# Attention's first tiles: r and k loaded without empty partitions, one v tile first, two products on VectorE, masks written ahead of the next tile's sums

## The chip, the cores and the metric

The kernel runs on one core of one Trainium2 chip. The metric is device time in microseconds (us) of one execution; three executions of the kernel before took 468.62, 472.92 and 474.53 us, median 472.92. The engines are PE (TensorE; PEld are its weight loads), DVE (VectorE), ACT (ScalarE), POOL (GpSimd) and SP (SyncE, which only issues DMAs here).

## The reference

Three layers follow one another: a decaying linear attention over 2 batches x 8 heads x 768 steps with head dimension 48, a mixture of 8 experts over 1536 tokens of 384, and a gated feed-forward layer.

```python
for t in range(S):                                   # attention, per batch and head
    cur = u * k[t] (outer) v[t]
    y[t] = r[t] @ (state + cur)
    state = w * state + k[t] (outer) v[t]
e = argmax(x @ w_gate)                               # experts: first `capacity` tokens of each
out[i] = gate_w[i] * (relu(x[i] @ w1[e]) @ w2[e])
out = (silu(x @ w_gate) * (x @ w_val)) @ w_out       # gated layer
```

## The kernel before

`attention` (L109 to L423) works on 12 tiles of 128 tokens, 6 of each batch. Inside a tile the recurrence is written as products: r and k are scaled by powers of the decay (`RK`), r against k gives a 128x128 matrix for each of 8 heads (`A`), which is masked and multiplied by v; what came before the tile enters through a state `Z` of 48x48 for each head.

Two layouts of r and k are loaded for a tile: `rkT`, with the head dimension on partitions (two heads at partitions 0 to 47 and 64 to 111; 48 to 63 and 112 to 127 are zero padding that the host writes, so 128 partitions are loaded), and `rk`, with the tokens on partitions. Both have three buffers. All these loads, and those of v (three tiles in one DMA), are issued by SP in program order; `u_b`, `wg` and `cap_i` are issued by ACT. A DMA signals its end on one of eight semaphores (DMAHW0 to DMAHW7), which SP and ACT share and which are used in turn: a DMA whose semaphore still belongs to an earlier one is issued when that one has landed.

Before the first tile a table `W2` of powers of w and of 1/w is built by doubling: w_dm lands, DVE clamps it into `sq` (L192), squares it seven times and fills the w half (L206, L207); POOL fills the 1/w half up to column 64 (L195, L211), DVE the last step. POOL has by then made the identity, the triangle `tmpm` and three index tables; DVE turns `tmpm` into the byte mask (L187) ahead of `sq`.

The work of a tile i is spread over the loop of L358, which runs `it` from -4, and each engine keeps the order in which the code is written:

- `decay(i)`: `RK[i]` = rkT x W2 on DVE (at it = i-3).
- `diag_pool(i)`: on POOL `ruk` = r x k (L236), `ruk` x u (L237), then `kd` = k x a row of W2 (L239; at it = i-4).
- `diag_dve(i)`: sums of `ruk` over each head, `c[i]` (L243); `diag_act(i)`: `AT[i]` = the identity times c, eight instructions on ACT (L252; both at it = i-3).
- `inner(i)`: `A` = products of `RK[i]` on PE, and then two masked copies on DVE (L266) that put A's upper triangle over `AT[i]` (at it = i-2). They need A and the finished `AT[i]`.
- `state_pe(i)`: `U` = kd against v on PE (L274, at it = i-2); `state_update`: Z on DVE and POOL.
- `outputs(i)` (PE), `d_major(i)` (`xT` on ACT, L312), `token_major(i)` (`xl` on PE, L449), and then the router and the scatter of the tokens into `x_disp` (at it = i and i+1).

So in one turn of the loop the sums of tile it+3 stand on DVE ahead of the masks of tile it+2. After the last tile `experts` (its first matmul is L750) and `gated` run, with their weights loaded ahead by SP.

Of the kernel before, what the change touches and what calls it, by code (L numbers as in the profile page):

```python
# [10 lines left out]
F32 = mybir.dt.float32  # L11
# [11 lines left out]
P = 128  # L23
B, H, S, D = 2, 8, 768, 48
# [3 lines left out]
DM = H * D  # L28
# [35 lines left out]
class Kernel:  # L64
# [44 lines left out]
    def attention(self, st):  # L109
        tc, nc, a = self.tc, self.nc, self.a  # L110
        tp = self.tp = self.pool(st, "tp")
        cp = self.cp
        ps_1 = self.ps_1 = self.pool(st, "ps_1", space=PSUM)
        NB = 3
# [3 lines left out]
        rkT = [tp.tile([P, 2, HP, P], F32, name=f"rkT{i}") for i in range(NB)]  # L118
        rk = [tp.tile([P, 2, DM], F32, name=f"rk{i}") for i in range(NB)]
        v_all = tp.tile([P, NT, DM], F32, name="v_all")  # L120

        def load_T(i):
            if i < NT:
                nc.sync.dma_start(out=rkT[i % NB], in_=a["rkT"][i])

        def load_rk(i):
            if i < NT:
                nc.sync.dma_start(out=rk[i % NB], in_=a["rk"][i])

        def load_v(i):  # L130
            nc.sync.dma_start(
                out=v_all[:, i:i + 3], in_=a["v"][i * P:(i + 3) * P].rearrange("(n p) d -> p n d", p=P)
            )

        load_T(0)
        load_rk(0)
        u_b = tp.tile([P, DM], F32, name="u_b")
# [2 lines left out]
        nc.scalar.dma_start(out=wg, in_=a["wg"].rearrange("p h e -> p (h e)"))  # L140
        cap_i = tp.tile([P, 2], I32, name="cap_i")
        nc.scalar.dma_start(out=cap_i, in_=a["cap"].bitcast(I32).partition_broadcast(P))
        load_v(0)
        load_T(1)
        load_rk(1)
        load_T(2)
        load_rk(2)


        ident = cp.tile([P, P], F32, name="ident")  # L150
# [5 lines left out]
        def warm(n):  # L156
# [7 lines left out]
            out=tmpm, in_=ones, pattern=[[1, P]], compare_op=ALU.is_gt, fill=0.0, base=0, channel_multiplier=-1  # L164
# [16 lines left out]
        for part in (y[:, 0:3], y[:, 3:], U):  # L181
# [6 lines left out]
        W2 = tp.tile([P, 2, HP, P], F32, name="W2")  # L188
# [11 lines left out]
            out=neq, in0=sq[:, 0], scalar=1.0, in1=w_dm, op0=ALU.mult, op1=ALU.not_equal, accum_out=nbad  # L200
# [3 lines left out]
        for i in range(7):  # L204
            n = 1 << i
# [4 lines left out]
            eng = nc.gpsimd if i < 6 else nc.vector  # L210
# [11 lines left out]
        RK, AT, cc, ruks = {}, {}, {}, {}  # L222
        xTs = self.xTs = {}
        self.xl, self.xu, self.batches, self.to_scatter = {}, {}, BATCHES, []
        self.row = cp.tile([P, NT], I32, name="row")

        def decay(i):
            RK[i] = tp.tile([P, 2, HP, P], F32, name="RK", tag="RK", bufs=4)

            for h in (slice(0, 2), slice(2, HP)) if i == 0 else (slice(0, HP),):  # L230
                nc.vector.tensor_mul(RK[i][:, :, h], rkT[i % NB][:, :, h], W2[:, :, h])

        def diag_pool(i):
            r_t, k_t = rk[i % NB][:, 0], rk[i % NB][:, 1]
            ruk = ruks[i] = tp.tile([P, DM], F32, name="ruk", tag="ruk", bufs=2)
            nc.gpsimd.tensor_mul(ruk, r_t, k_t)  # L236
            nc.gpsimd.tensor_mul(ruk, ruk, u_b)  # L237
            if i % NCH < NCH - 1:
                nc.gpsimd.tensor_mul(kds[i % NB], k_t, wk_tok)  # L239

# [47 lines left out]
        def outputs(i):  # L288

            for hp in range(HP):  # L290
                for j in range(2):
                    rows = slice(64 * j, 64 * j + D)
                    z = self.zero[rows, 0:D] if i % NCH == 0 else Z[i % 2][rows, hp]
                    nc.tensor.matmul(
                        y[rows, hp], lhsT=z, rhs=RK[i][rows, 0, hp],
                        start=(hp == 0), stop=False, skip_group_check=True,
                    )
            for hp in range(HP):
                for j in range(2):
                    nc.tensor.matmul(  # L300
                        y[64 * j:64 * j + D, hp], lhsT=head(v_all, i, 2 * hp + j), rhs=AT[i][:, j, hp],
                        start=False, stop=True, skip_group_check=True,
                    )

        def d_major(i):
            xT = xTs[i] = tp.tile([P, HP, P], F32, name="xT", tag="xT", bufs=2)
            if i in self.last:

                nc.vector.tensor_copy(xT[:, 0:2], y[:, 0:2])
                nc.scalar.copy(xT[:, 2:], y[:, 2:])  # L310
            else:
                nc.scalar.copy(xT, y)  # L312
            del RK[i], AT[i]
# [41 lines left out]
        ok = lambda i: 0 <= i < NT  # L355
        has_state = lambda i: ok(i) and i % NCH < NCH - 1
        ends = {hi - 1: (lo, hi) for lo, hi in BATCHES}
        for it in range(-4, NT + 1):  # L358
            batch = ends.get(it - 1)
            if ok(it):  # L360
                outputs(it)
                d_major(it)
            if ok(it - 1):
                self.logits(it - 1)
            if batch:
                self.route1(*batch)
            if it == NT:
                first_add(NT - 2, False, False)
                self.place_pe(*batch)
                first_rows(False)  # L370
            if has_state(it + 1):
                state_update(it + 1)
            if it == NT:
                self.route2(*batch)
                first_add(NT - 1, False, True)
            if it < 0 and ok(it + 3):
                decay(it + 3)
                load_T(it + 3 + NB)
            if ok(it + 3):
                diag_dve(it + 3)  # L380
                diag_act(it + 3)
            if ok(it + 4):
                diag_pool(it + 4)
                load_rk(it + 4 + NB)
            if ok(it + 2):
                inner(it + 2)
            if it == NT - 1:
                first_add(NT - 3, True, False)
            if batch and it < NT:
                self.place_pe(*batch)  # L390
            if it >= 0 and ok(it + 3):
                decay(it + 3)
                load_T(it + 3 + NB)
            if batch and it < NT:
                self.route2(*batch)
            for _ in range(2 if it == NT - 2 else 1):
                if self.to_scatter and it < NT:
                    self.scatter()
            if it == -3:
                late_tables()  # L400
            if it in (-1, 2, 4):
                load_v({-1: 3, 2: 6, 4: 9}[it])
            if it in (-2, 0):
                first = (it + 2) // 2 * ST
                self.clear_rows(self.x_disp[first:first + BLK])
            if ok(it):
                self.token_major(it)
            if has_state(it + 2):
                state_pe(it + 2)
            if it == NT - 2:  # L410
                self.x_load(0, self.xr0)
            if it >= 3:
                self.prefetch(it - 3)
            if it in WARMS:
                warm(WARMS[it])
# [690 lines left out]
def layout(inp):  # L1106
    r, k, v = (np.asarray(inp[n]) for n in "rkv")
    tok = lambda x: x.transpose(0, 2, 1, 3).reshape(N, DM)
    o = {}

    def pad(x):

        z = np.zeros(x.shape[:2] + (64,) + x.shape[3:], x.dtype)
        z[:, :, :D] = x
        return z.reshape((x.shape[0], P) + x.shape[3:])


    dm = lambda x: x.reshape(B, HP, 2, NCH, P, D).transpose(0, 3, 2, 5, 1, 4).reshape(NT, 2, D, HP, P)
    o["rkT"] = pad(np.stack([dm(r), dm(k)], axis=3))
    o["rk"] = np.ascontiguousarray(np.stack([tok(r).reshape(NT, P, DM), tok(k).reshape(NT, P, DM)], axis=2))  # L1120
    o["v"] = np.ascontiguousarray(tok(v))
    w = np.asarray(inp["w"])
    o["w_dm"] = pad(w.reshape(1, HP, 2, D).transpose(0, 2, 3, 1))[0]
    o["w_row"] = np.ascontiguousarray(w.reshape(DM))
    o["u_row"] = np.ascontiguousarray(np.asarray(inp["u"]).reshape(DM))
    o["wg"] = pad(np.asarray(inp["moe_w_gate"]).reshape(1, HP, 2, D, E).transpose(0, 2, 3, 1, 4))[0]
    o["cap"] = np.asarray(inp["moe_capacity"], dtype=np.int64).reshape(1)
    w1 = np.asarray(inp["moe_w1"])
    o["w1"] = np.ascontiguousarray(w1.reshape(E, KD, P, 4, 256).transpose(0, 3, 2, 1, 4)).reshape(E, 4, P, UC)
    w2 = np.asarray(inp["moe_w2"])  # L1130
    o["w2"] = np.ascontiguousarray(w2.reshape(E, 4, 2, P, DM).transpose(0, 1, 3, 2, 4)).reshape(E, 4, P, UC)
    for n in ("w_gate", "w_val"):
        m = np.ascontiguousarray(np.asarray(inp["moe2_" + n], dtype=np.float64))
        o[n] = np.ascontiguousarray(
            m.view(np.int64).reshape(KD, P, 6, 256).transpose(2, 1, 0, 3)
        ).reshape(6, P, KD * 256)
    m = np.ascontiguousarray(np.asarray(inp["moe2_w_out"], dtype=np.float64))
    o["w_out"] = np.ascontiguousarray(m.view(np.int64).reshape(6, 2, P, DM).transpose(0, 2, 1, 3)).reshape(6, P, 2 * DM)
    return o
# [17 lines left out]
```

## Time and profile before

| what | us |
|---|---|
| three executions | 468.62, 472.92, 474.53 (median 472.92) |
| the profiled execution, its own time | 468.19 |
| its span, first to last instruction | 466.4 |
| busy in the span: PE, PEld | 439.6, 424.0 |
| busy: DVE, ACT, POOL | 293.2, 211.5, 179.0 |
| first matmul of the experts starts at | 95.53 |

The profiled execution is 1.0% under the median of the three. Times in the rows are us from the span's start. A row's duration is that of all instructions it merges; the bracket at its end is the engine's idle time before it, and what ended it.

### The profile page before, as it was taken

Reading aid. Unit: us, or ns where it says so; the run is one execution under the profiler, and the core shown is the slowest. Engines: PE = TensorE matmul, PEld = TensorE weight load, DVE = VectorE, ACT = ScalarE, POOL = GpSimd, SP = SyncE. Lnnn points to the kernel's source line nnn. Section 1 sums busy time; section 2 is a strip of 40 time slices with the busy share of each in tenths; the row PEclk is TensorE's granted clock in tenths of the full one; section 3 lists DMA queues with packets and bytes.
Section 4 is the critical chain, followed back from the end, with each engine's and each line's share of the span. In section 5 each row is a group of like instructions: output and inputs, shape, how many; then the busy total and the mean of one; then the engine's idle time right before and its main releaser. Section 6 shows DMA issues by size and latency. Waiting matters only on the chain. (4 is left out here: it accounts for less than half of the span.)

```text
span 466.4 us, 8409 instructions
## 1 busy us (share of the span) xinstructions
PE 439.6 (94%) x3204; PEld 424.0 (91%) x3204; DVE 293.2 (63%) x567; ACT 211.5 (45%) x468; POOL 179.0 (38%) x161
## 2 busy tenths in 40 slices
PE   7898978799999999999999999999999999999991
PEld 6677866698999999999999999999999999999991
DVE  5679777568797788889465697989857111111110
ACT  2666654254675675666455554344244032130310
POOL 5995962221122102100044445665454433233331
PEclk9899889789999999999999999999999999999996
DMA  7697750549998999750202423324300000100001
GB/s 264 248 320 240 274 209 36 173 113 314 353 316 223 252 255 263 244 200 1 69 1 67 133 82 126 113 91 135 117 20 1 34 19 0 52 0 35 18 19 39
DMA packets 24802, 63.78 MB, mean 137 GB/s; under 512 B 4784, under 2 KB 10032, under 8 KB 24752
## 3 DMA queue, kind: packets, MB, share of 16 engines
q1 hardware_dynamic: 22112, 57.43, 38.6%
q0 software_dynamic: 1920, 4.73, 2.8%
q10 hardware_dynamic: 720, 1.00, 0.8%
q8 instruction: 27, 0.44, 0.4%
q14 instruction: 23, 0.19, 0.1%
HBM read 55.67 MB, written 7.48 MB: 135 GB/s over the span
## 5 line engine op out<-in xcount | busy, mean ns | idle before, releaser
L960 POOL TENSOR_TENSOR al<-sg,ah 128x384 fp32r<-128x384 f32 x48 | 54.3, 1131 | 122.5 <-ACT ah L959 122.4
L593 DVE TENSOR_TENSOR wlo<-raw,whi 128x768 fp32r<-128x768 f32 x60 | 58.2, 970 | 9.6 <-ACT whi L592 9.5
L727 PE MATMUL py<-hc,whi 128*128 128x448 f32 x192 | 63.1, 370 | 0.0
L959 ACT CAST ah<-sg 128x384 fp32r<-128x384 f32 x48 | 24.7, 515 | 78.2 <-DVE sg L956 78.2
L738 PE MATMUL A<-xc,whi 128*128 128x224 f32 x336 | 57.4, 275 | 0.8 <-DVE xc L609 0.7
L728 PE MATMUL py<-hc,wlo 128*128 128x256 f32 x192 | 53.8, 280 | 0.0
L738 PEld LDWEIGHTS A<-xc,whi 128*128 128x128 f32 x336 | 51.1, 192 | 1.5 <-DVE xc L609 1.1
L592 ACT CAST whi<-raw 128x768 fp32r<-128x768 f32 x60 | 49.8, 837 | 0.7 <-PE py L727 0.7
L973 PE MATMUL po<-w_out_hi,ah 128*128 128x384 f32 x144 | 48.6, 337 | 0.0
L975 PE MATMUL po<-w_out_hi,al 128*128 128x384 f32 x144 | 48.5, 337 | 0.0
L974 PE MATMUL po<-w_out_lo,ah 128*128 128x384 f32 x144 | 48.5, 337 | 0.0
L738 PE MATMUL A<-xc,wlo 128*128 128x224 f32 x168 | 46.1, 275 | 0.0
L982 DVE TENSOR_TENSOR acc<-acc,po 128x384 f32<-128x384 f32 x36 | 19.3, 546 | 30.9 <-PE po L975 30.9
L727 PEld LDWEIGHTS py<-hc,whi 128*128 128x128 f32 x192 | 36.0, 188 | 2.5
L803 POOL DMA_INDIRECT ids<-tok,by_expert x12 | 14.0, 1169 | 60.9 <-DMA ids<-tok,by_expert 60.6
L956 DVE TENSOR_TENSOR sg<-A,sg 128x384 f32<-128x384 f32 x24 | 13.3, 555 | 38.0 <-PE A L953 30.3
L728 PEld LDWEIGHTS py<-hc,wlo 128*128 128x128 f32 x192 | 36.5, 190 | 0.0
L956 DVE TENSOR_TENSOR sg<-g,sg 128x384 f32<-128x384 f32 x24 | 13.3, 555 | 34.5 <-PE g L953 27.6
L252 ACT ACTIVATE AT<-ident,c 128x128 f32<-128x128 f32 x96 | 29.4, 392 | 7.6 <-DVE c L243 7.5
L757 ACT ACTIVATE hc<-A 128x224 fp32r<-128x224 f32 x64 | 23.1, 362 | 21.3 <-PE A L738 18.0
L738 PEld LDWEIGHTS A<-xc,wlo 128*128 128x128 f32 x168 | 32.2, 192 | 0.0
L955 ACT ACTIVATE sg<-A 128x384 f32<-128x384 f32 x24 | 11.7, 486 | 34.7 <-PE A L953 34.7
(172 smaller groups left out, 1137.3 us busy)
## 6 DMA issues: line engine op xcount, KB each, us to landing
raw<-in_w SPq DMA_DIRECT2D x62, 384.0 KB, 6.5
rkT<-in_rkT SPq DMA_DIRECT2D x12, 512.0 KB, 5.5
rk<-in_rk SPq DMA_DIRECT2D x12, 384.0 KB, 4.2
raw<-in_w_gate SPq DMA_DIRECT2D x6, 768.0 KB, 4.2
raw<-in_w_val SPq DMA_DIRECT2D x6, 768.0 KB, 5.0
raw<-in_w_out SPq DMA_DIRECT2D x6, 768.0 KB, 4.2
x_disp<-zero SPq DMA_DIRECT2D x8, 336.0 KB, 6.1
xr<-x_disp SPq DMA_DIRECT2D x8, 336.0 KB, 6.0
```

Of the source, the lines that this page charges most:

```text
L252: nc.scalar.activation(AT[i][:, j, hp], ident, AF.Copy, scale=c[:, j, hp:hp + 1])
L592: nc.scalar.copy(h_, raw)
L593: nc.vector.tensor_sub(l_, raw, h_.bitcast(F32))
L727: nc.tensor.matmul(ps[:, 0:2 * BLK], lhsT=wh, rhs=xc, start=first, stop=False, skip_group_check=True)
L728: nc.tensor.matmul(ps[:, 0:256], lhsT=wl, rhs=xc[:, 0:256], start=False, stop=last, skip_group_check=True)
L738: self.nc.tensor.matmul(ph[:, HI], lhsT=w[:, k, fs], rhs=x[1][:, k, half], start=(k == 0 and i == 0), stop=(k == KD - 1 and i == 2),)
L956: nc.vector.tensor_mul(sg, pg["w_val"], sg)
L959: nc.scalar.copy(h_, sg)
L960: nc.gpsimd.tensor_sub(l_, sg, h_.bitcast(F32))
L973: nc.tensor.matmul(po, lhsT=ah[:, ts_], rhs=wh, start=(i == 0), stop=False)
L974: nc.tensor.matmul(po, lhsT=ah[:, ts_], rhs=wl, start=False, stop=False)
L975: nc.tensor.matmul(po, lhsT=al[:, ts_], rhs=wh, start=False, stop=(i == len(parts) - 1))
```

## The change

1. The host no longer pads rkT. `load_T` issues two DMAs of 48 partitions each, 192 KB apiece, in place of one of 512 KB. POOL zeroes partitions 32 to 63 of the three buffers first of all, and `RK` is computed on partitions 0 to 111.
2. `load_v` takes a count: v's first tile is loaded alone, after rkT 1; the next two after rk 2.
3. For tile 0 the two products of `ruk` run on DVE, behind `decay(0)`, and rk 3 is loaded behind them (after rkT 3).
4. While it < 0, `inner(it + 2)` stands ahead of `diag_dve(it + 3)`; from it = 0 on, the old order holds.

```diff
         def load_T(i):
             if i < NT:
-                nc.sync.dma_start(out=rkT[i % NB], in_=a["rkT"][i])
+                for j in range(2):
+                    nc.sync.dma_start(out=rkT[i % NB][64 * j:64 * j + D], in_=a["rkT"][i, j])
...
-        def load_v(i):
+        def load_v(i, n=3):
             nc.sync.dma_start(
-                out=v_all[:, i:i + 3], in_=a["v"][i * P:(i + 3) * P].rearrange("(n p) d -> p n d", p=P)
+                out=v_all[:, i:i + n], in_=a["v"][i * P:(i + n) * P].rearrange("(n p) d -> p n d", p=P)
             )
 
+        for t in rkT:
+            nc.gpsimd.memset(t[32:64], 0.0)
         load_T(0)
         load_rk(0)
...
-        load_v(0)
         load_T(1)
+        load_v(0, 1)
         load_rk(1)
         load_T(2)
         load_rk(2)
+        load_v(1, 2)
...
+        hd = slice(0, 64 + D)
         def decay(i):
...
-                nc.vector.tensor_mul(RK[i][:, :, h], rkT[i % NB][:, :, h], W2[:, :, h])
+                nc.vector.tensor_mul(RK[i][hd, :, h], rkT[i % NB][hd, :, h], W2[hd, :, h])
+        def diag_product(eng, i):
+            ruk = ruks[i] = tp.tile([P, DM], F32, name="ruk", tag="ruk", bufs=2)
+            eng.tensor_mul(ruk, rk[i % NB][:, 0], rk[i % NB][:, 1])
+            eng.tensor_mul(ruk, ruk, u_b)
         def diag_pool(i):
-            r_t, k_t = rk[i % NB][:, 0], rk[i % NB][:, 1]
-            ruk = ruks[i] = tp.tile([P, DM], F32, name="ruk", tag="ruk", bufs=2)
-            nc.gpsimd.tensor_mul(ruk, r_t, k_t)
-            nc.gpsimd.tensor_mul(ruk, ruk, u_b)
+            k_t = rk[i % NB][:, 1]
+            if i:
+                diag_product(nc.gpsimd, i)
...
             if it < 0 and ok(it + 3):
                 decay(it + 3)
                 load_T(it + 3 + NB)
+                if it == -3:
+                    diag_product(nc.vector, 0)
+                    load_rk(NB)
+            if it < 0 and ok(it + 2):
+                inner(it + 2)
             if ok(it + 3):
                 diag_dve(it + 3)
                 diag_act(it + 3)
             if ok(it + 4):
                 diag_pool(it + 4)
-                load_rk(it + 4 + NB)
-            if ok(it + 2):
+                if it > -4:
+                    load_rk(it + 4 + NB)
+            if it >= 0 and ok(it + 2):
                 inner(it + 2)
```

The order on POOL at the start, in the changed kernel (the first row is the last thing the kernel before has ahead of `ident`, too):

```order
5 L1171 UNCONDITIONAL_BRANCH
6 L138 MEMSET rkT_84 32x1024
7 L138 MEMSET rkT_85 32x1024
8 L138 MEMSET rkT_86 32x1024
9 masks.py:197 MEMSET ident 128x128
10 masks.py:199 ISA
11 masks.py:199 AFFINE_SELECT ident<-ident 128x128
12 L168 AFFINE_SELECT tmpm<-ones 128x128
```

The three memsets are new and stand ahead of the identity and of `tmpm`.

DVE from the first `RK` to the third sums, in the kernel before (`RK` x2 is tile 0 in two halves; `c` are the sums, `AT` the masks):

```order
31 L231 TENSOR_TENSOR RK<-rkT_84,W_146 128x2x256 x2
32 L243 TENSOR_REDUCE c<-ruk 128x4x2
33 L330 COPY Wm<-sq 128x192
34 L435 COPY IW<-ident 128x4x48 x2
40 L231 TENSOR_TENSOR RK<-rkT_85,W_146 128x1024
41 L243 TENSOR_REDUCE c<-ruk 128x4x2
42 L266 COPY_PREDICATED AT<-mask,A 128x512 x2
43 L282 TENSOR_TENSOR Z_136<-U,Wm 112x192
44 L231 TENSOR_TENSOR RK<-rkT_86,W_146 128x1024
45 L243 TENSOR_REDUCE c<-ruk 128x4x2
46 L266 COPY_PREDICATED AT<-mask,A 128x512 x2
```

The same stretch in the changed kernel:

```order
31 L238 TENSOR_TENSOR RK<-rkT_84,W_153 112x2x256 x2
32 L242 TENSOR_TENSOR ruk<-rk_87 128x384
33 L243 TENSOR_TENSOR ruk<-ruk,u_b 128x384
34 L254 TENSOR_REDUCE c<-ruk 128x4x2
35 L341 COPY Wm<-sq 128x192
42 L238 TENSOR_TENSOR RK<-rkT_85,W_153 112x1024
43 L277 COPY_PREDICATED AT<-mask,A 128x512 x2
44 L254 TENSOR_REDUCE c<-ruk 128x4x2
45 L293 TENSOR_TENSOR Z_143<-U,Wm 112x192
46 L238 TENSOR_TENSOR RK<-rkT_86,W_153 112x1024
47 L277 COPY_PREDICATED AT<-mask,A 128x512 x2
48 L254 TENSOR_REDUCE c<-ruk 128x4x2
```

The products of tile 0 are in, and the masks of tiles 0 and 1 have changed places with the sums of tiles 1 and 2.

SP's first DMAs in the changed kernel, with the semaphores each waits for before it is issued:

```order
2 L125 DMA rkT_84<-in_rkT 48x1024 [waits Pool_49]
3 L125 DMA rkT_84<-in_rkT 48x1024
4 L129 DMA rk_87<-in_rk 128x768
5 L125 DMA rkT_85<-in_rkT 48x1024 [waits Pool_49]
6 L125 DMA rkT_85<-in_rkT 48x1024 [waits DMAHW0_49]
7 L132 DMA v_all<-in_v 128x384 [waits DMAHW1_49]
8 L129 DMA rk_88<-in_rk 128x768 [waits DMAHW2_49]
9 L125 DMA rkT_86<-in_rkT 48x1024 [waits DMAHW3_49,Pool_49]
10 L125 DMA rkT_86<-in_rkT 48x1024 [waits DMAHW4_49]
11 L129 DMA rk_89<-in_rk 128x768 [waits DMAHW5_49]
12 L132 DMA v_all<-in_v 128x2x384 [waits DMAHW6_49]
```

Each buffer's first half waits for its memset on POOL (Pool_49). The eight semaphores come round sooner: DMAHW0 is that of `u_b`, DMAHW2 that of `wg`, DMAHW4 that of `cap_i`. In the kernel before rk 1 is the first that waits, for DMAHW0.

## Rows read from the trace of the kernel before

**Rows 1.** Busy time by stretch: length, then each engine; granted clock, DMA share, GB/s.

```profile
5.00:10.00 5.00, 4.25 (x38) 3.58 (x37) 2.85 (x13) 0.48 (x1) 3.31 (x6) 1.00 0.99 367
10.00:15.00 5.00, 3.55 (x29) 3.20 (x29) 2.94 (x10) 2.45 (x8) 4.13 (x4) 0.69 1.01 397
15.00:20.00 5.00, 3.99 (x64) 3.42 (x64) 3.78 (x7) 2.46 (x9) 4.92 (x5) 0.97 0.57 204
...
25.00:30.00 5.00, 4.13 (x68) 3.50 (x64) 4.04 (x7) 3.80 (x12) 4.92 (x5) 1.00 0.93 315
...
80.00:85.00 5.00, 5.00 (x40) 4.12 (x40) 1.66 (x9) 0.68 (x3) 1.52 (x2) 0.66 0.12 43
90.00:95.00 5.00, 4.51 (x17) 4.37 (x18) 1.03 (x6) 0.35 (x1) 0.96 (x1) 0.54 0.64 230
100.00:300.00 200.00, 198.23 (x1359) 194.29 (x1358) 156.76 (x247) 116.30 (x242) 52.66 (x37) 1.00 0.58 177
```

**Rows 2.** Instructions in order of time, POOL and DVE to the first `RK`: start, duration.

```profile
0.82 0.20 POOL masks.py:197 MEMSET ident<- 128x128 f32 x1 [0.29 <-POOLq L1147]
...
1.68 0.24 DVE L187 CAST mask<-tmpm 128x128 uint8<-128x128 f32 x1 [0.18 <-POOL tmpm L163]
1.70 0.14 POOL L171 IOTA tok<- 128x12 f32 x1
...
1.80 0.34 POOL L173 IOTA slot<- 128x224 f32 x1
...
3.61 0.17 DVE L192 TENSOR_SCALAR sq<-w_dm 128x4 f32<-128x4 f32 x1 [1.69 <-DMA w_dm<-in_w_dm]
...
6.63 0.42 DVE L211 TENSOR_TENSOR W<-W,iq 128x256 f32<-128x256 f32 x1 [0.58 <-POOL W L211]
...
7.17 1.29 DVE L231 TENSOR_TENSOR RK<-rkT,W 128x512 f32<-128x512 f32 x2
```

**Rows 3.** Instructions in order of time, tiles 0 to 2 on POOL, DVE and ACT.

```profile
7.98 1.34 POOL L236 TENSOR_TENSOR ruk<-rk 128x384 f32<-128x384 f32 x1 [1.38 <-DMA rk<-in_rk]
...
9.40 0.99 POOL L237 TENSOR_TENSOR ruk<-ruk,u_b 128x384 f32<-128x384 f32 x1
...
10.42 0.56 DVE L243 TENSOR_REDUCE c<-ruk 128x8 f32<-128x384 f32 x1 [1.96 <-POOL ruk L237]
...
11.01 2.45 ACT L252 ACTIVATE AT<-ident,c 128x128 f32<-128x128 f32 x8 [2.73 <-DVE c L243]
...
12.13 2.09 POOL L236 TENSOR_TENSOR ruk<-rk 128x384 f32<-128x384 f32 x1 [0.79 <-DMA rk<-in_rk]
12.21 1.15 DVE L231 TENSOR_TENSOR RK<-rkT,W 128x1024 f32<-128x1024 f32 x1
...
15.33 0.55 DVE L243 TENSOR_REDUCE c<-ruk 128x8 f32<-128x384 f32 x1 [1.96 <-POOL ruk L237]
15.80 1.35 DVE L266 COPY_PREDICATED AT<-mask,A 128x512 f32<-128x512 uint8 x2
...
19.40 0.55 DVE L243 TENSOR_REDUCE c<-ruk 128x8 f32<-128x384 f32 x1 [0.89 <-POOL ruk L237]
...
22.34 0.56 ACT L312 COPY xT<-y 128x512 f32<-128x512 f32 x1
```

**Rows 4.** DMA issues, of `wg` at 1.27 and rk 1 at 5.60: KB, us to landing.

```profile
wg<-in_wg ACTq DMA_DIRECT2D x1, 16.0 KB, 5.9
...
rk<-in_rk SPq DMA_DIRECT2D x1, 384.0 KB, 6.5
```

**Rows 5.** Waits of SP's queue to 10 us: total, times, longest.

```profile
SPq L128 <- DMA u_b<-in_u_row: 2.2, 1, 2.2
```

**Rows 6.** Instructions in order of time: v of tiles 3 to 5, and the experts' first matmul.

```profile
23.72 0.45 SPq L131 DMA_DIRECT2D v_all<-in_v  x1
...
29.63 0.56 PE L274 MATMUL U<-v_all,kd 128*48 128x48 f32 x16 [0.86 <-DMA v_all<-in_v]
...
95.53 0.72 PE L750 MATMUL A<-x_plain,raw 128*128 128x224 f32 x1
```

More of the change, by code (lines that the diff above doesn't have):

```diff
@@ L1118, in layout @@
     dm = lambda x: x.reshape(B, HP, 2, NCH, P, D).transpose(0, 3, 2, 5, 1, 4).reshape(NT, 2, D, HP, P)
-    o["rkT"] = pad(np.stack([dm(r), dm(k)], axis=3))
+    o["rkT"] = np.ascontiguousarray(np.stack([dm(r), dm(k)], axis=3))
     o["rk"] = np.ascontiguousarray(np.stack([tok(r).reshape(NT, P, DM), tok(k).reshape(NT, P, DM)], axis=2))
```

## The prediction

> **What bounds the kernel now.** I read the busy time by stretch first, then the instructions in order of time over the first 30 us, then the waits. From 100 us on PE is busy 198.23 of 200 us at full granted clock [rows 1]; nothing in the change touches that part, so all that can be won or lost is the time at which the experts' first matmul starts, 95.53 [rows 6]. A gain of 2% of 472.9 is 9.5 us, a tenth of all that comes before it.
>
> Three things set the pace early. To 7.17 it is the building of W2: sq starts at 3.61, when w_dm has landed, and the first `RK` starts at 7.17, right behind the table's last step at 6.63 [rows 2]. The next is the chain of tile 0: rk 0 lands at 7.98, POOL's two products (1.34 and 0.99) end at 10.39, the sums c0 stand at 10.42, AT0 at 11.01 for 2.45 [rows 3]. From 12.13, when rk 1 has landed, it is POOL: 4.92 busy of 5 between 15 and 20 and again between 25 and 30 [rows 1]. Beside it DMA has a share of 0.99 and 1.01 from 5 to 15 [rows 1], so that rk 1, issued at 5.60, takes 6.5 to land [rows 4]. At 29.63 PE has waited 0.86 for v of tiles 3 to 5, issued at 23.72 [rows 6], behind a load that waits for POOL to finish the third `kd`.
>
> **The change part by part.**
>
> *Memsets.* Three memsets of 1024 elements a partition now precede ident and tmpm on POOL. The trace has none of that length. Lower end: 0.20 each, the memset of 128 elements [rows 2], if length hardly counted. Upper end: 2.64, POOL's product at its 0.99 for 384 elements [rows 3] times 1024/384. I take a value near the first: from 12 to 224 elements an iota grows from 0.14 to 0.34 [rows 2], 0.94 ns an element, so 0.95 for a memset, 2.85 for three. The mask, at 1.68 right behind tmpm [rows 2], moves to 1.68 + 2.85 = 4.53. It stands ahead of sq on DVE, so sq starts at about 4.7, 1.1 later than 3.61. The w_dm wait hides the first 1.8 of it, the rest is on the path. `RK` 0 moves from 7.17 to 8.25 and ends at 9.55 (1.29). rkT 0 waits for its memset, about 0.5 later than now, and its bytes are fewer; it is in time for 8.25.
>
> *Products of tile 0 on DVE.* DVE has a row of 384 elements, the sums, at 0.56, and `RK`'s halves of 512 at 0.65 [rows 2, 3]; I take 0.53 each, 1.06. They end at 10.6 and c0 moves from 10.42 to 10.6: what POOL's 2.33 gave is spent by the memsets. With memsets of 0.20 nothing before sq is late and c0 stands at 7.17 + 1.29 + 1.06 = 9.5.
>
> *Loads.* A tile's rkT shrinks from 524 to 393 thousand bytes, and the first v from 590 to 197. Ahead of rk 1 that is 2 x 131 + 393 = 655 thousand fewer, at 397 GB/s [rows 1] 1.65 us. But rkT 0 starts 0.5 later, and rk 1 is issued when its semaphore is free: now it waits 2.2 for u_b [rows 5] and goes out at 5.60; then it waits for wg, issued at 1.27 and 5.9 on its way [rows 4], so to 7.2 or a little less. With a shorter queue before it, it lands near 11.1 instead of 12.13. If it kept its 6.5 [rows 4] it would land at 13.7: the late end.
>
> *POOL.* It runs only kd 0 for tile 0, from about 9.3 (the row of W2 comes 1.1 later, too). A POOL product beside a DVE product is held up: 2.09 against 0.99 while `RK` 1 runs for 1.15 [rows 3]. kd 0 lies beside the products of tile 0 and ends near 11.2. Tile 1's products begin at 11.2 instead of 12.13; kd 1 ends 0.9 earlier, and so does what POOL does up to kd 3, since POOL is the bound there.
>
> *Masks ahead of sums.* Mask 0 needs AT0, done at 10.6 + 0.6 + 2.45 = 13.7; now it starts at 15.80 behind c1 [rows 3], then at 13.7, 2.1 earlier, which brings nothing by itself: PE reaches tile 0's outputs later. c1 comes behind it at 13.7 + 1.35 = 15.05, 0.3 before its 15.33. AT1 then ends at 18.1, mask 1 at 19.45, and c2, which now stands behind mask 1, at 19.45 against 19.40 [rows 3]: no gain. A serial chain of 0.6 + 2.45 + 1.35 = 4.4 us for a tile has taken POOL's place. ACT's xT 0 follows AT2 and stays near 22.34, and PE's tile 0 behind it. Zero for tiles 0 to 2.
>
> *Where a gain appears.* From it = 0 the old order holds and POOL's 0.9 counts again. The load ahead of v's tiles 3 to 5 is issued 0.9 earlier, and the 0.86 that PE waits at 29.63 [rows 6] shrinks to 0.2, as each load also moves less. I put it at 0.7.
>
> *RK on 112 partitions* costs the same (elements per partition are unchanged). A second rkT issue a tile, some 0.4 us on SP, is covered: in the rows read SP waits on POOL or on a semaphore, not the reverse.
>
> **Sum:** 0 to the third tile, -0.7 at 29.63, carried to the experts' start: 95.53 becomes 94.8. The profiled execution, 468.2 for a span of 466.4, would take 467.5. The median, 472.9, would become 472.2; the mean of the four executions, 471.1, would become 470.4. I predict between these, **471.3**.
>
> **One rule against the rows.** The DMA share of 1.0 at 367 to 397 GB/s [rows 1] is that of loads over 128 partitions; my 1.65 us holds if two halves run at that rate together. The Trainium skill, "SBUF — State Buffer on-chip working memory", section "Door 1: The DMA port swizzle", says that partitions 0 to 63 reach only 8 of 16 ports, so that a load of one half runs at about half the rate (196 GB/s against 328), and that two at once hardly help (+6%). No row here shows a half-height load; its price for this kernel is the second rival's.
>
> **Rivals.**
>
> 1. *The memsets are dear.* One mechanism: POOL's memset delays tmpm, mask, sq and the table. Each 0.1 above 0.95 puts 0.3 on c0, c1 and c2, one for one along the serial chain. From 0.95 + 0.7/3 = 1.2 us each the kernel is slower than before. At 1.9 it is 2.85 - 0.7 = 2.1 slower, 475.0; at the upper end of 2.64 it is 5.1 - 0.7 = 4.4 slower, 477.3. For it: POOL's products take 2.6 ns an element. Against: its iota takes 0.94.
> 2. *The halves run one after the other.* At half of 397 GB/s rkT takes 2.0 us instead of 1.3. Ahead of rk 1 two such pairs cost 1.3 more and the smaller v saves 1.0, with the late start 0.5: rk 1 lands near 12.9, POOL's 0.9 is gone, v of tiles 3 to 5 is no earlier: +0.3, 473.2. What the skill's rule says would do this; DMA's share is below 1 after 15 us, 0.57 to 20, so that there it would be covered.
> 3. *The memsets are cheap*, 0.20 to 0.4. Then c0 comes 0.9 earlier, c1 1.2 (mask 0 ends at 14.0), c2 1.0, and v's wait goes as well: -1.6, 470.4 by the same reckoning as the forecast's 471.3.
>
> **How the numbers follow.** Forecast 0.50, dear memsets 0.15, halves one after the other 0.20, cheap memsets 0.15. All lie within 5 us of no change. To this comes what shifts with the start: PE's granted clock is 0.66 from 80 to 85 and 0.54 from 90 to 95 [rows 1], near the lower of its levels, 1.2 of 2.4 GHz, and a shift of some tenths can add or spare such a stretch, about 1 to 2 us. And the executions shown differ by 6 us. The range is 466.0 to 475.6: from the cheap memsets on a run as quick as the profiled one to memsets of about 1.9 on the median. Two per cent, about 9.5 us, is what a measurement can tell from no change: faster 0.03, same 0.94, slower 0.03.
>
> **What would show it.** Memset rows near 0.95 and sq near 4.7; `RK` 0 near 8.25; two DVE products before c0 at 10.6; rk 1 landed near 11.1; mask 0 near 13.7 and c2 near 19.4, now waiting behind mask 1; U of tile 3 with less than 0.3 of a wait for v; the experts' first matmul near 94.8. I am wrong if sq is not delayed, if rk 1 lands after 12.13, or if the experts' start moves by more than 2 us.

## The result and the profile after

The changed kernel takes 474.09 us (median of 20 executions, 472.71 to 479.89); the kernel before, run beside it, 472.18 (20, 468.47 to 476.34). The ratio is **1.0078, 95% interval 1.0053 to 1.0103**: 3.7 us slower. This and every ratio below leaves out executions more than 1.5% above the fastest of their kernel (3 of 20 before, 1 of 20 after); the medians don't, and so differ from them. The time lies in the range given, and within 2% of before; the sign is not the one forecast.

The profiled execution after took 473.37 us (span 471.7), the one before 468.19 (span 466.4). Its start, in order of time on POOL and DVE, with one row of PE (start, duration, engine, line, operation; the bracket is idle time before it):

```profile
0.83 2.72 POOL L138 MEMSET rkT<- 32x1024 f32 x3 [0.29 <-POOLq L1165]
...
4.61 0.34 DVE L197 TENSOR_SCALAR sq<-w_dm 128x4 f32<-128x4 f32 x1
...
8.26 1.29 DVE L238 TENSOR_TENSOR RK<-rkT,W 112x512 f32<-112x512 f32 x2
...
9.53 1.34 POOL L250 TENSOR_TENSOR kd<-rk,wk_tok 128x384 f32<-128x384 f32 x1 [1.76 <-ACT wk_tok L225]
10.05 1.23 DVE L243 TENSOR_TENSOR ruk<-ruk,u_b 128x384 f32<-128x384 f32 x1
...
11.32 0.55 DVE L254 TENSOR_REDUCE c<-ruk 128x8 f32<-128x384 f32 x1
11.46 1.00 POOL L242 TENSOR_TENSOR ruk<-rk 128x384 f32<-128x384 f32 x1 [0.59 <-DMA rk<-in_rk]
11.79 0.78 DVE L341 COPY Wm<-sq 128x192 f32<-128x192 f32 x1
...
12.50 1.21 DVE L453 COPY IW<-ident 128x192 f32<-128x192 f32 x2
12.54 1.06 POOL L243 TENSOR_TENSOR ruk<-ruk,u_b 128x384 f32<-128x384 f32 x1
13.56 1.01 POOL L250 TENSOR_TENSOR kd<-rk,wk_tok 128x384 f32<-128x384 f32 x1
13.63 0.97 DVE L457 COPY IW<-wg 128x32 f32<-128x32 f32 x1
14.52 0.21 DVE L458 CAST before<-tmpm 128x128 bf16<-128x128 f32 x1
14.53 1.06 POOL L242 TENSOR_TENSOR ruk<-rk 128x384 f32<-128x384 f32 x1
14.65 0.95 DVE L459 CAST rev<-rev_i 128x8 f32<-128x8 int32 x1
...
15.73 1.16 DVE L238 TENSOR_TENSOR RK<-rkT,W 112x1024 f32<-112x1024 f32 x1
16.81 1.32 DVE L277 COPY_PREDICATED AT<-mask,A 128x512 f32<-128x512 uint8 x2
...
17.03 2.62 PE L270 MATMUL A<-RK 48*128 48x128 f32 x16 [4.00 <-DVE RK L238]
...
18.04 0.53 DVE L254 TENSOR_REDUCE c<-ruk 128x8 f32<-128x384 f32 x1
```

To 8.26 this is the forecast. Then read the pairs from 11.46 on: rk 1 is there earlier than before (12.13 in [rows 3]), so POOL multiplies without a pause from 11.46, and four of the copies on DVE end within 0.15 us of the end of a POOL product (12.57 and 12.46, 13.71 and 13.60, 14.60 and 14.57, 15.60 and 15.59), one of 32 columns taking 0.97 us and two of 192 together 1.21. The same copies before, while POOL was idle from 11.34 to 12.13:

```profile
11.38 0.42 DVE L435 COPY IW<-ident 128x192 f32<-128x192 f32 x2
...
11.72 0.17 DVE L439 COPY IW<-wg 128x32 f32<-128x32 f32 x1
```

The second `RK` starts at 15.73 instead of 12.21 [rows 3].

The same windows as [rows 1] (length, busy time of PE, PEld, DVE, ACT, POOL, granted clock, DMA share, GB/s):

```profile
5.00:10.00 5.00, 4.36 (x34) 3.87 (x35) 4.43 (x28) 0.48 (x1) 2.52 (x8) 1.00 1.01 284
10.00:15.00 5.00, 2.58 (x38) 2.14 (x34) 4.93 (x9) 2.45 (x8) 4.33 (x5) 1.00 1.06 304
15.00:20.00 5.00, 2.97 (x26) 2.70 (x28) 5.00 (x9) 1.40 (x5) 4.84 (x5) 0.66 1.00 268
25.00:30.00 5.00, 4.58 (x72) 4.03 (x72) 3.28 (x6) 3.60 (x12) 3.12 (x5) 1.00 0.93 268
```

At a DMA share of 1.0 the engines move 268 to 304 GB/s; in [rows 1] they moved 367 to 397. The share from 15 to 20 is 1.00 instead of 0.57: the queue has no slack there. The granted clock of 15 to 20 is 0.66 (0.97 before), after PE waited 4.00 us for the second `RK`; part of that stretch is at 1.2 of 2.4 GHz.

SP's queue (q1) in the first 40 us, and behind it the scatters of routed tokens from 40 to 75 (packets, MB, share of 16 engines; then KB and median us to landing). Before:

```profile
q1 hardware_dynamic: 4257, 10.67, 76.7%
...
q1 hardware_dynamic: 2431, 6.14, 50.0%
...
x_disp<-xu,row POOLq DMA_INDIRECT x6, 3.5
```

After:

```profile
q1 hardware_dynamic: 3935, 9.06, 80.6%
...
q1 hardware_dynamic: 2577, 6.18, 61.3%
...
x_disp<-xu,row POOLq DMA_INDIRECT x5, 6.3
```

10.67 MB in 76.7% of 40 us are 348 GB/s while busy; 9.06 MB in 80.6% are 281. Fewer bytes take more time, and from 40 to 75, as many bytes take 61.3% instead of 50.0%. The scatters share the engines. Their two medians, 3.5 and 6.3 us, are not of the same scatters: the window holds six before and five after, which start later. One by one, the first three land in 4.4, 5.0 and 7.6 us before and in 6.3, 7.6 and 7.1 after; the next takes 2.6 and 3.7. Waits for them, 40 to 110 (total, times, longest), before:

```profile
POOL x_disp L527 <- DMA x_disp<-xu,row: 4.7, 2, 2.4
...
ACT xu L458 <- DMA x_disp<-xu,row: 0.5, 1, 0.5
```

And after:

```profile
ACT xu L476 <- DMA x_disp<-xu,row: 7.7, 4, 4.2
POOL x_disp L545 <- DMA x_disp<-xu,row: 7.6, 3, 3.3
```

Where it ends up in these two executions: the last scatter, the load of `xr` that reads what was scattered, and PE's transposes of it (`px`), which stand among the first expert's matmuls. Before:

```profile
95.53 0.72 PE L750 MATMUL A<-x_plain,raw 128*128 128x224 f32 x1
...
100.26 0.96 POOL L527 DMA_INDIRECT x_disp<-xs,row  x1 [2.47 <-DVE wlo L593]
...
103.73 0.33 SPq L601 DMA_DIRECT2D xr<-x_disp  x1
109.40 0.74 PE L719 MATMUL px<-ident,xr 112*128 112x112 f32 x6
```

After:

```profile
97.81 1.52 PE L768 MATMUL A<-x_plain,raw 128*128 128x224 f32 x5
...
104.17 0.96 POOL L545 DMA_INDIRECT x_disp<-xs,row  x1 [4.09 <-DVE wlo L611]
...
107.84 0.34 SPq L619 DMA_DIRECT2D xr<-x_disp  x1
...
114.41 0.80 PE L737 MATMUL px<-ident,xr 112*128 112x112 f32 x6 [3.09 <-DMA xr<-x_disp]
```

The experts' start moves by 2.3 (95.53 to 97.81), and `px` by 5.0, with a wait of 3.09 that wasn't there. From `px` to the end of the span it is 357.0 before and 357.3 after; in the fourteen profiles of this study 356.8 to 359.1. What `px` loses, the kernel loses. But a landmark of a single profile moves from one execution to the next: in two profiles of one and the same kernel (`e_full_tables`, below) the experts' first matmul starts at 96.85 and at 93.45. And the profile before is of an execution 4 us under the median of its kernel, the one after of one near it. So the sizes below come from the timed ratios, and a profile says where only what other profiles repeat.

### The profile page after: what moved, and what is told of

Same layout as the page of the kernel before. It is cut to its first block, busy times and chain, and to the rows that moved or that the text cites. A ratio compares the mean times of both kernels' runs of the same rounds, so it can differ in the third digit from the quotient of the medians.

```text
span 471.7 us, 8442 instructions
## 1 busy us (share of the span) xinstructions
PE 438.4 (93%) x3204; PEld 423.6 (90%) x3204; DVE 300.2 (64%) x569; ACT 211.8 (45%) x468; POOL 177.1 (38%) x162
## 5 line engine op out<-in xcount | busy, mean ns | idle before, releaser
L745 PE MATMUL py<-hc,whi 128*128 128x448 f32 x192 | 64.6, 377 | 0.0
L821 POOL DMA_INDIRECT ids<-tok,by_expert x12 | 13.7, 1139 | 61.1 <-DMA ids<-tok,by_expert 52.7
```

The source lines that it names most:

```text
L745: nc.tensor.matmul(ps[:, 0:2 * BLK], lhsT=wh, rhs=xc, start=first, stop=False, skip_group_check=True)
```

## The experiments

Three theories: **tables** (A: POOL's products hold up DVE's copies, the first tiles are late), **halves** (B: loads of half height slow the DMA engines, and with them the scatters and `xr`), **memsets** (C: they delay the decay table).

### Whole loads, tables on ACT, and both

`e_full_load` undoes halves and memsets:

```diff
-                for j in range(2):
-                    nc.sync.dma_start(out=rkT[i % NB][64 * j:64 * j + D], in_=a["rkT"][i, j])
+                nc.sync.dma_start(out=rkT[i % NB], in_=a["rkT"][i])
...
-        for t in rkT:
-            nc.gpsimd.memset(t[32:64], 0.0)
...
-    o["rkT"] = np.ascontiguousarray(np.stack([dm(r), dm(k)], axis=3))
+    o["rkT"] = pad(np.stack([dm(r), dm(k)], axis=3))
```

> The changed kernel with rkT loaded as before (one DMA over 128 partitions, padding from the host, no memsets); the other parts stay. Theory A (DVE's late tables are held up by POOL's products): sq back near 3.6, c0 near 9.6, but the tables still take 2.5 us or more instead of 1.3, decay 1 starts after 13.5, and about 1 us of the loss stays. Theory B (half-height loads slow the DMA engines, scatters land late, ACT waits for them): the scatters of 40 to 75 us land in 3.5 us again instead of 6.3, ACT's wait for them falls from 7.7 us to below 1, and at least 2 of the 3.7 us come back. Theory C (memsets alone): 1.1 us comes back and nothing else moves. Time by A+B: 471.5 to 473, by A alone 473 to 474.5.

`e_tables_act` is the changed kernel with the late tables copied by ACT behind `wk_tok`; `e_full_tables` has both edits.

```diff
+        self.route_rooms()
+        nc.scalar.copy(Wm, sq[:, 7].unsqueeze(2).to_broadcast([P, HP, D]))
+        self.route_tables(wg, tmpm, rev_i, cap_i, nc.scalar.copy)
...
-            nc.vector.tensor_copy(Wm, sq[:, 7].unsqueeze(2).to_broadcast([P, HP, D]))
-            self.route_tables(wg, tmpm, rev_i, cap_i)
```

> The changed kernel with the late tables (Wm, IW, before, rev, cap_f) copied by ACT, behind wk_tok, in place of DVE. Theory A: decay 1 starts near 11.9 instead of 15.73, PE is not idle from 13 to 17, outputs of tile 0 start near 18 instead of 20.39, experts' first matmul at 96.5 or before, time 1 to 2 below the changed kernel: 472 to 473. Theory B (the DMA engines, slowed by the half loads, set the pace later): the early gain is there but gone by the experts' start; time as the changed kernel, 474 to 475.

> Both of the two: rkT loaded over 128 partitions without memsets, and the late tables on ACT. A and B together: 1 to 2.5 below the kernel before, 469.5 to 471; experts' first matmul near 94. If the loss has another cause (the mask order, the products on DVE): no better than the kernel before, 472 or more.

Measured against before: whole loads **1.0006** (0.9963 to 1.0050), tables on ACT **1.0050** (1.0009 to 1.0091), both **0.9972** (0.9933 to 1.0011). Whole loads give the loss back, although their tables are still slow and the second `RK` is at 15.06. Their queue to 40 us, and ACT's waits for scatters from 40 to 110:

```profile
q1 hardware_dynamic: 4154, 10.48, 76.4%
...
ACT xu L473 <- DMA x_disp<-xu,row: 4.9, 3, 2.3
```

The rate is 343 GB/s while busy, as before. But theory B expected these waits to fall below 1, and they are 4.9 with the loss gone. Of `e_tables_act`, DVE in order of time:

```profile
11.32 0.55 DVE L257 TENSOR_REDUCE c<-ruk 128x8 f32<-128x384 f32 x1
...
11.93 1.51 DVE L241 TENSOR_TENSOR RK<-rkT,W 112x1024 f32<-112x1024 f32 x1
```

The second `RK` is back where it was, 3.8 us earlier than in the changed kernel, and tile 0's outputs on PE start at 16.42 instead of 20.39; the time moves by 0.3%, and the intervals overlap. Behind whole loads the same edit moves it by 0.3% as well (1.0006 to 0.9972), and again the intervals overlap. The lateness of the first tiles is real; that it costs at most a part of the loss is what these runs say, not how much.

### Memsets

`e_memsets` is the kernel before with three memsets of spare tiles ahead of `ident`; `e_hidden` is the changed kernel with its first memset on DVE, behind that of `ones` alone, and the others on POOL behind the index tables; the loads of tiles 1 and 2 stand behind these in the code.

```diff
+        spare = [tp.tile([P, 2, HP, P], F32, name=f"spare{i}") for i in range(3)]
+        for t in spare:
+            nc.gpsimd.memset(t[32:64], 0.0)
```

> The kernel before with three memsets of spare tiles on POOL ahead of the identity, nothing else. Theory C: three rows near 0.91, sq near 4.6 instead of 3.61, first RK near 8.26, c0 0.6 to 1.1 later than 10.42, time 0.5 to 1.1 above the kernel before. Theories A and B: the memsets are not the main part, less than 1.2 of the 3.7 us.

```diff
-        for t in rkT:
-            nc.gpsimd.memset(t[32:64], 0.0)
+        ones = tp.tile([P, P], F32, name="ones")
+        nc.vector.memset(ones, 1.0)
+        nc.vector.memset(rkT[0][32:64], 0.0)
...
         nc.gpsimd.iota(slot, pattern=[[1, BLK]], base=0, channel_multiplier=0, allow_small_or_imprecise_dtypes=True)
+        for t in rkT[1:]:
+            nc.gpsimd.memset(t[32:64], 0.0)
```

> The changed kernel with its three memsets taken off the path: the first buffer's is on VectorE ahead of everything else there, the other two are on POOL behind its index tables, where POOL waits anyway. The loads stay in halves. Every theory: the triangle and the mask are early again, sq starts near 3.6 and the first RK near 7.3. Memsets theory (they cost what the change lost): the changed kernel's loss goes, 472.2, level with the kernel before. Halves theory (loads of 48 partitions slow the DMA queue and the scatters): the gain is only what the 1.1 us of sq brings on tile 0, mostly absorbed by the tables and the products behind it, 473.5 to 474; bytes of SP's queue to 40 us stay near 281 GB/s while it is busy, and the scatters' landing stays near 6 us.

`e_memsets`: **1.0104** (1.0013 to 1.0196, from four executions), sq at 4.61, c0 at 11.25. `e_hidden`: **1.0074** (1.0038 to 1.0110). DVE and POOL of `e_hidden`:

```profile
3.39 0.73 DVE L198 TENSOR_SCALAR sq<-w_dm 128x4 f32<-128x4 f32 x1 [0.19 <-DMA w_dm<-in_w_dm]
...
7.43 1.29 DVE L239 TENSOR_TENSOR RK<-rkT,W 112x512 f32<-112x512 f32 x2
...
11.13 0.42 DVE L454 COPY IW<-ident 128x192 f32<-128x192 f32 x2
...
11.97 1.83 DVE L239 TENSOR_TENSOR RK<-rkT,W 112x1024 f32<-112x1024 f32 x1
```

Here memsets and slow tables are both gone (rk 1 came a little later, at 11.68, so the copies were done first), and the loss is whole. They are not what the changed kernel pays for. Whether memsets alone cost something stays open: the interval of `e_memsets` lies above 1, but it is wide and rests on four executions.

### One load of 112 partitions

`e_112` loads rkT with one DMA of partitions 0 to 111 from an array with the middle gap padded, without memsets; `e_112_tables` has the tables on ACT as well.

```diff
-                for j in range(2):
-                    nc.sync.dma_start(out=rkT[i % NB][64 * j:64 * j + D], in_=a["rkT"][i, j])
+                nc.sync.dma_start(out=rkT[i % NB][0:64 + D], in_=a["rkT"][i])
```

> The changed kernel with rkT loaded by one DMA over 112 partitions (the 16 empty ones between the heads still come from the host), and so without the memsets. Products on VectorE, the small v and the mask order stay. Halves theory: the DMA rate is that of the whole load (about 348 GB/s to 40 us) though 16 partitions fewer are moved, scatters land in 3.5 to 4 us, and the time is that of the version with the whole 128 partitions, 471.8, or a few tenths less for the fewer bytes: 471.4 to 471.9. A rival, that fewer than 128 partitions in a load is itself what is slow (the ports not all reached alike): near the changed kernel's 474.

> A version meant to beat both: one load of 112 partitions, no memsets, and the tables needed late (Wm, IW, before, rev, cap) copied by ACT instead of VectorE, where POOL's products of tiles 1 and 2 hold them up. Theory on the tables: the second RK starts near 11.4 instead of 15, tile 0's outputs near 16 instead of 20, and the kernel takes 1.2 us less than the one load of 112 partitions alone, 470.3, or 1.9 us under the kernel before. Rival: what the first tiles win is taken back at the first batch of tokens, where the router's work on VectorE and the scatters set the pace: level with the one load of 112 partitions, 471.5.

`e_112`: **1.0030** (0.9994 to 1.0065); `e_112_tables`: **1.0038** (1.0002 to 1.0075). SP's queue to 40 us in `e_112`:

```profile
q1 hardware_dynamic: 4014, 9.88, 86.2%
```

That is 287 GB/s while busy, the rate of the halves, against 343 of `e_full_load`. The rival named there holds for the rate: 112 partitions are enough to lose it. For the time it is not shown: 1.0030 is less than half of the changed kernel's loss, the interval holds 1, and it also overlaps that of the changed kernel. Whether the slow rate alone brings the whole loss is thus open, and a rival stands: the second DMA of each tile, with its issue and its semaphore, which every version with two loads has as well. With the tables on ACT nothing was won, as its rival said.

### The order and the products, each alone

`e_order` is the kernel before with the fourth part alone, `e_products` with the third alone (diffs as in the change).

> The kernel before with the fourth part alone: while it < 0 the masks stand ahead of the next tile's sums. Prediction's view: mask 0 can start when AT0 is done at 13.5, not 15.80, brings nothing to tile 0's outputs, c1 a little earlier or later; no change, 472 +- 1. Rival: c1 behind mask 0 waits for A on PE and is later, so AT1, mask 1 and c2 are later, and the first tiles lose up to 1 us: 473.

> The kernel before with the third part alone: tile 0's two products on VectorE behind its RK, rk 3 loaded behind them; loads, v and order as before. Halves theory (only the loads' shape makes the loss): no loss, 0.998 to 1.003. Theory on the tables: rk 1 lands as late as before (12.1), so POOL still idles while VectorE copies the tables, they stay near 1.3 us in all and the second RK stays near 12.2 to 12.6; c0 comes at 10.4 to 10.9, the second product held to 1.2 by POOL's kd. Rival (the products on VectorE are themselves what makes the first tiles late): the second RK near 14 or later and 1 to 2 us lost, 1.003 to 1.005.

`e_order`: **0.9998** (0.9954 to 1.0041). c1 stays at 15.31 and c2 at 19.29 (15.33 and 19.40 in [rows 3]). `e_products`: **1.0020** (0.9981 to 1.0060); its copies run free, since rk 1 lands at 12.11 as before, and the second `RK` starts at 11.87. Neither part moves the time beyond its interval, which leaves room for 0.4% and 0.6%.

### Halves alone, and halves late

`e_halves64` is the kernel before with its padded rkT in two loads of 64 partitions, the same bytes. `e_late48` is `e_full_load` with halves of 48 from tile 3 on.

```diff
-                nc.sync.dma_start(out=rkT[i % NB], in_=a["rkT"][i])
+                for j in range(2):
+                    nc.sync.dma_start(out=rkT[i % NB][64 * j:64 * j + 64], in_=a["rkT"][i, 64 * j:64 * j + 64])
```

> The kernel before with one edit: rkT, padded as it was, comes in two loads of 64 partitions instead of one of 128, the same bytes, no memsets, nothing moved on any engine. Halves theory: the 4096-byte packets of rkT take near 240 ns instead of 173, SP's queue is busy longer for the same bytes, the scatters of x_disp land later, the last of them and the load of xr behind it are 3 to 4 us late, and the kernel takes 3 to 4 us more than before: ratio 1.006 to 1.009. Rival (the halves only hurt where the first tiles are late too, through memsets and tables): within 1 us of before.

```diff
-                nc.sync.dma_start(out=rkT[i % NB], in_=a["rkT"][i])
+                if i < NB:
+                    nc.sync.dma_start(out=rkT[i], in_=a["rkT"][i])
+                for j in range(2 if i >= NB else 0):
+                    nc.sync.dma_start(out=rkT[i % NB][64 * j:64 * j + D], in_=a["rkT"][i, 64 * j:64 * j + D])
```

> The version with whole loads (471.8 by its own runs), except that tiles 3 to 11 come in halves of 48 partitions, 25% fewer bytes; tiles 0 to 2 come whole, so nothing is different before 20 us. If the halves cost by making the first tiles late: no change against the whole loads, 471.8. If they cost by slowing the queue between 20 and 60 us, where the weights and the scatters come behind them: near the changed kernel, 473.5 to 474.5.

`e_halves64`: **1.0088** (1.0046 to 1.0130). `e_late48`: **1.0055** (1.0016 to 1.0094). SP's queue to 40 us and the scatters from 40 to 75 in `e_halves64`:

```profile
q1 hardware_dynamic: 4023, 9.68, 90.6%
...
x_disp<-xu,row POOLq DMA_INDIRECT x4, 7.4
```

One edit, not an instruction moved on a compute engine, and the loss is there, with 267 GB/s while busy and `px` at 115.25. (7.4 is the median of the three scatters whose landing is on record; they took 6.1, 7.4 and 7.8.) The sign is firmer than the size: the two medians are only 0.8 us apart (474.52 and 473.74). In `e_late48` the first three tiles come whole and the first half is issued at 8.81 (tile 3), so the expectation's "nothing is different before 20 us" was wrong. Its interval lies above 1, as the halves of later tiles would have it, but overlaps that of `e_full_load`; which tiles' loads cost how much is not shown.

Do the scatters carry the loss? Theory B has it so, and the pair of profiles at the start looks like it; others don't. `e_tables_act` has halves, 287 GB/s to 40 us and first scatters of 6.0, 7.1 and 7.2 us; `e_memsets` has whole loads, 347 GB/s and 2.7, 4.9 and 6.5. Their `px`:

```profile
110.01 0.79 PE L738 MATMUL px<-ident,xr 112*128 112x112 f32 x6 [0.59 <-DMA xr<-x_disp]
...
113.22 0.79 PE L722 MATMUL px<-ident,xr 112*128 112x112 f32 x6 [2.32 <-DMA xr<-x_disp]
```

The slow scatters go with the early `px`, and the quick ones with the late. What repeats in all fourteen profiles is the rate of the queue to 40 us: 343 to 356 GB/s in the seven with whole loads, 267 to 287 in the six without, 317 in `e_late48`.

### The combination once more

> The version with whole loads and the tables on ACT once more, for a narrower interval (first: 0.9972 of before, 0.9933 to 1.0011). If moving the tables is worth 1.3 us behind whole loads: 0.995 to 0.999. Rival (what the first tiles win is taken back by the time of the last scatter): 0.999 to 1.002.

Whole loads and tables on ACT again: **0.9980** (0.9932 to 1.0028). Both medians of this version are lower than those of before beside it (470.62 and 471.69; 472.16 and 473.74), and both intervals hold 1. It beats the changed kernel (0.9972 and 0.9980 against 1.0078, and the intervals do not meet); that it beats the kernel before is not shown.

## Why the prediction was wrong, step by step

- **Memsets: right.** 0.907 us each against 0.95; sq 4.61 (4.7), `RK` 0 at 8.26 (8.25).
- **Products of tile 0: short by 0.7.** The second took 1.23, not 0.53, because POOL's `kd` 0 ran from 9.53 to 10.87. I priced POOL held up by DVE, not DVE by POOL; c0 came at 11.32, not 10.6.
- **Loads and POOL: the landing right, what follows wrong.** rk 1 was at POOL at 11.46 (11.1 to 11.2), and the wait for v of tile 3 is gone, as forecast, though that matmul now starts at 31.16 and not before 29.63. But POOL's earlier start was booked as 0.9 won, without asking what DVE does then: the late tables, 10.89 to 12.21 before, took from 11.79 to 15.73. The Trainium skill, "SBUF — State Buffer", section "Who interferes with whom", has DVE's fast copies and POOL exclude each other over a shared pair of ports, the later one blocked; the ends of copies and products above agree. So mask 0 was at 16.81 (13.7), c2 at 21.89 (19.45). With the tables on ACT this lateness is gone, and of the loss 0.5% stays (`e_tables_act`, 0.1 to 0.9%).
- **Masks ahead of sums, `RK` on 112 partitions: right, zero** within what can be told (`e_order`, give or take 0.4%; 1.16 against 1.15).
- **Halves: the step that failed.** The forecast took two halves at the rate of a whole load. The rule weighed there held in its direction: 281 against 348 GB/s. My second rival had the slower rate, with 0.20, and failed on place: it priced rk 1's landing, which was not late, and called the rest "covered" because one window showed a share of 0.57. [Rows 1] itself has 0.93 from 25 to 30, and q1 was busy 76.7% of the first 40 us: a fifth slower, the same bytes would fill 95%. It gave +0.3 us; the halves alone cost 0.88% (0.46 to 1.30), some 4 us by the ratio.
- **The landmark.** I let the experts' first matmul stand for the end. In the pair of profiles it moved by 2.3; `px`, 14 us later, by 5.0, and there PE waits 3.09 for the load of `xr`. I had not followed the scatters at all.
- **The range.** That 474.09 lies in it is no merit: its upper part was there for dear memsets and for the spread of the executions, not for slower loads.

So two things are shown: loads of less than 128 partitions slow the queue, and splitting rkT into two loads makes the kernel slower. What lies between, from the slower queue to a later `px`, is open: scatters and `xr` are late in the changed kernel's profile, but in `e_tables_act` and `e_memsets` the scatters and `px` go opposite ways. Nor was the first v tried alone.

## What to carry to other kernels

Count a DMA by the engine time it takes, not by its bytes: leaving out a quarter of the partitions moved 1.6 MB less in the first 40 us and made the queue busier. Before calling a slower transfer covered, look at the queue's share over the whole stretch in which it is used and at who else lands through those engines. Before taking a chain from one pair of profiles, look whether other profiles with the same cause show its middle links. When an engine is let off a wait, look at which instructions of its neighbour had been running in that wait.

## What was not expected of the hardware

- A load of 112 partitions is as slow as two halves: SP's queue moves 287 GB/s while busy, against 343 to 356 with 128. In its packet records to 40 us a 4096-byte packet takes a median of 212 ns (159 with 128 partitions; 229 in the changed kernel, 271 in `e_halves64`), and 3072-byte packets, those of rk, itself unchanged, 152 ns in `e_112` and 125 in the changed kernel instead of 121.
- Beside POOL's products of 1.0 us, a DVE copy of 128x32 takes 0.97 us instead of 0.17, and one of two times 128x192 1.21 instead of 0.42.
- POOL zeroes 32 partitions of 1024 elements in 0.907 us, 0.89 ns an element.
